# All of the first 21 slots' attention weights transposed by TensorE, and the loads on the GpSimd queue issued earlier

## The chip, the cores and the metric

The kernel runs on one core of a Trainium2 chip. The metric is the device time of one execution in microseconds; the kernel before took 562.66 us in the median of five runs (561.29 to 563.73). The engines are named as in the profile: PE (TensorE matmul), PEld (its weight loads), DVE (VectorE), ACT (ScalarE), POOL (GpSimd) and SP (SyncE, here only a queue that issues DMAs).

## The reference, cut to what matters

```python
def _attn_ref(q, k, v, tau):                      # (8, 8, 576, 64)
    scale = 1.0 / np.sqrt(q.shape[-1])
    scores = scale * np.matmul(q, k.transpose(0, 1, 3, 2))
    thresh = np.max(scores, axis=-1, keepdims=True) - tau
    scores = np.where(scores >= thresh, scores, -1000000000.0)
    scores = scores - np.max(scores, axis=-1, keepdims=True)
    attn = np.exp(scores)
    attn = attn / (np.sum(attn, axis=-1, keepdims=True) + 1e-09)
    return np.matmul(attn, v)

def _moe_ref(x, w_in, w_out):                     # (4608, 512), (512, 2048), (2048, 512)
    h = x @ w_in
    relu6 = np.clip(h + 3.0, 0.0, 6.0)
    g = h * relu6 / 6.0
    return g @ w_out
```

The output of the attention, with its heads side by side, is the input x of the second part. "Attention weights" below are the normalized `attn`; "projection weights" are w_in and w_out.

## The kernel before, in words

**Tiling.** The 64 heads are taken in 32 pairs; two pairs are a quad, two quads a batch. A quad has nine slots: slots 0 to 3 are the four blocks of 128 queries of its first pair, 4 to 7 those of its second, and slot 8 holds the remaining 64 queries of both. In a slot both heads of a pair are worked on, so every tile has two halves of 128 x 576. All 16 quads make a queue of 144 slots, numbered n = 0 to 143 here; n = 9 x quad + slot.

**One slot.** The loop at line 434 issues, in this order: the exponentials of the slot before (line 290, ACT); the row maxima of this slot (line 277, DVE, which also copies the scores out of PSUM) and the biases made of them (line 280, POOL, two tiny instructions); from n = 22 on a piece of the second part's first product (line 353 PE, 362 ACT or 364 DVE, 370 DVE); the transposes by TensorE of the slot two before, where it is marked `on_chip` (line 314, nine matmuls into the PSUM tile `pt`, one buffer of the pool `ps_h`, and line 315, their eviction on DVE); the reciprocal of the slot before (line 293, DVE); a piece of the second product (line 382); the masks of this slot (line 285, ACT); a transpose of q or k for the next pair or quad (line 213, 231) or a product with the values (`av`, lines 323 and 326); the scores of the next slot (lines 256 and 262, PE, into `ps_s`, two buffers); the warm-up (line 164, six PE transposes of an identity whose result nobody reads, n < 8); the normalization of the slot before (line 298, POOL, two instructions of 128 x 576); and at its end the transfers.

**Order.** The order is written out by hand. Every engine takes its instructions in the order of issue, so an instruction that waits holds all behind it on its engine. Where the eviction stands in the order of DVE is set by line 462: behind the reciprocal, ahead of the evictions of q and k.

**The two ways of a transpose.** The attention weights `pn` must be transposed before the product with v. A slot marked `on_chip` has it done by TensorE and DVE as told; any other slot gives one DMA transpose to SP's queue (line 306). In the kernel before the odd slots of the first 21 are marked: n = 1, 3, ... 19, ten slots.

**The queues.** SP's queue carries the loads of q and k (lists `loads`, one job a slot, each of several DMAs, lines 88, 92 and 107), the DMA transposes and the stores (line 403). POOL's queue carries what has to be cast to bf16 on the way: the values, four pieces a batch (list `vcasts`: two `vm` pieces of line 121 and two `vr` pieces of line 125), and the projection weights, 32 pieces (list `casts`: 16 of w_in, line 142, then 16 of w_out, line 146). POOL issues these in order with its biases and normalizations. The first batch's value pieces are in the list from the start; those of batch b + 1 are put there in slot 0 of the second quad of batch b, which is n = 9 for the second batch.

**When they are issued, before.** A value piece is started in a slot when n < 4 or n > 12, so the second batch's four go in slots 13 to 16. A weight piece is started in each slot from 4 to 23, and two in each slot from 24 to 29.

Of the kernel before, what the change touches and what calls it, by code (L numbers as in the profile page):

```python
# [21 lines left out]
def kernel(  # L22
# [20 lines left out]
    N1 = 22  # L43
# [31 lines left out]
    casts = []  # L75
    vcasts = []
# [3 lines left out]
    def load_quad(quad):  # L80
        b, g = divmod(quad, 2)
        nat[quad] = (nat_pool.tile([P, 1152], F32, tag="nq", name="nq"),
                     nat_pool.tile([P, 4, 4, D], F32, tag="km", name="km"),
                     nat_pool.tile([P, 2 * D], F32, tag="kr", name="kr"))
        nq, km, kr = nat[quad]

        def main(dst, src, h, order):
            nc.sync.dma_start(out=dst[:, :, h, :], in_=src[b, 4 * g + h, 0:512, :].rearrange(order, t=4))

        def blocks_q(n, a, j):  # L90
            c = 32 * (2 * a + j)
            nc.sync.dma_start(out=nq[c:c + 32, n * S:(n + 1) * S].rearrange("p (k d) -> p k d", d=32),
                              in_=q[b, 4 * g + 2 * n + a, :, 32 * j:32 * j + 32].rearrange("(k r) d -> r k d", r=32))

        def load_q(n):
            if b < NB:
                for a in range(2):
                    main(nq[:, 0:1024].rearrange("p (t h d) -> p t h d", h=4, t=4), q, 2 * n + a, "(t p) d -> p t d")
            else:
                for a in range(2):  # L100
                    for j in range(2):
                        blocks_q(n, a, j)

        def rest():
            for dst, src in ((kr[:], k), (nq[:, 1024:1152], q))[0:2 if b < NB else 1]:
                for n in range(2):
                    nc.sync.dma_start(out=dst[64 * n:64 * n + 64, :].rearrange("p (h d) -> p h d", h=2),
                                      in_=src[b, 4 * g + 2 * n:4 * g + 2 * n + 2, 512:S, :].rearrange("h p d -> p h d"))

        for n in range(2):  # L110
            loads.append(lambda n=n: [main(km, k, 2 * n + a, "(p t) d -> p t d") for a in range(2)])
            loads.append(lambda n=n: load_q(n))
            if n == 0:
                loads.append(rest)

    def load_v(b):
        vm = v_pool.tile([P, H, 4 * D], BF16, tag="vm", name="vm")
        vr = vrs[b % 2]
        vsb[b] = (vm, vr)
        for g in range(2):  # L120
            vcasts.append(lambda g=g: nc.gpsimd.dma_start(
                out=vm[:, g * 4:g * 4 + 4, :],
                in_=v[b, g * 4:g * 4 + 4, 0:512, :].rearrange("h (p t) d -> p h (t d)", t=4)))
        for a in range(2):
            vcasts.append(lambda a=a: nc.gpsimd.dma_start(
                out=vr[a * 64:(a + 1) * 64, a, :, :],
                in_=v[b, :, 512:S, :].rearrange("(hp a) p d -> a p hp d", a=2)[a]))
# [21 lines left out]
    def start(jobs, n):  # L149
        for _ in range(min(n, len(jobs))):  # L150
            jobs.pop(0)()
# [9 lines left out]
    def warm_up(count):  # L161
        warm = ps_h.tile([P, 2, 512], F32, tag="h", name="warm")
        for _ in range(count):
            nc.tensor.transpose(warm[:, 0, 0:P], identf[:], identf[:])
# [105 lines left out]
    def sm_max(sl):  # L270
        sl.s = s_pool.tile([P, 2, S], F32, tag="s", name="s")
        sl.m = stat_pool.tile([P, 2], F32, tag="m", name="m")
        sl.bias = stat_pool.tile([P, 2], F32, tag="bias", name="bias")
        sl.rsum = stat_pool.tile([P, 2], F32, tag="rsum", name="rsum")
        sl.rinv = stat_pool.tile([P, 2], F32, tag="rinv", name="rinv")
        for i, ps in enumerate(sl.tiles):
            nc.vector.tensor_scalar(out=sl.s[:, i, :].rearrange("p (a b) -> p a b", a=2), in0=ps[:, :, 0:HALF],  # L277
                                    scalar1=1.0, scalar2=None, op0=Alu.mult, op1=Alu.max,
                                    accum_out=sl.m[:, i:i + 1])
            nc.gpsimd.tensor_scalar(out=sl.bias[:, i:i + 1], in0=sl.m[:, i:i + 1], scalar1=-scale, scalar2=tau,  # L280
                                    op0=Alu.mult, op1=Alu.add)
# [6 lines left out]
    def sm_exp(sl, i):  # L288
        s = sl.s[:, i, :]
        nc.scalar.activation(out=s, in_=s, func=Act.Exp, accum_out=sl.rsum[:, i:i + 1])  # L290
# [67 lines left out]
    def mm1_relu(hps, on_act):  # L358
        w = hps.shape[2]
        r = r_pool.tile([P, 2, 320], F32, tag="r", name="r")[:, :, 0:w]  # L360
        if on_act:
            nc.scalar.activation(out=r, in_=hps, func=Act.Relu, bias=three[:])  # L362
        else:
            nc.vector.tensor_scalar(out=r, in0=hps, scalar1=3.0, scalar2=0.0, op0=Alu.add, op1=Alu.max)  # L364
        return r
# [58 lines left out]
    queue = []  # L424
    for quad in range(NQUAD):
        for slot in range(NSLOT):
            sl = Slot()
            sl.quad, sl.slot = quad, slot
            sl.on_chip = len(queue) < N1 - 1 and len(queue) % 2 == 1
            queue.append(sl)  # L430
    queue[0].tiles = scores(0, 0)

# [1 line left out]
    for n, sl in enumerate(queue):  # L434
        quad, slot = sl.quad, sl.slot
        b, g = divmod(quad, 2)
        now = n
        if slot in (0, 4):
            pts[2 * quad + slot // 4] = pt_pool.tile([P, 9, 512], BF16, tag="pT", name="pT")
        if slot == 8:  # L440
            ptr[quad] = ptr_pool.tile([P, 9, P], BF16, tag="pR", name="pR")
        if quad == 0 and slot == 0:
            load_quad(1)
        if slot == (4 if quad else 8) and quad + 2 < NQUAD:
            load_quad(quad + 2)
        if slot == 0 and g == 1 and b + 1 < B:
            load_v(b + 1)
        if prev is not None:
            for i in range(2):
                sm_exp(prev, i)  # L450
        sm_max(sl)

        if slot != 8 and todo1:
            item, then = todo1.pop(0)
            h = mm1(item)
            r = mm1_relu(h, on_act=(slot in (0, 1, 3, 5)))
            mm1_gate(item, h, r)
            todo2.extend(then)
        copies = pe_transpose(queue[n - 2]) if n > 1 and queue[n - 2].on_chip else None
        if prev is not None:  # L460
            sm_recip(prev)
        if copies:
            copies()
        outs = []


        pieces = 0 if slot == 3 else 1
        if slot == 0:
            second = True
        if second and slot < 2 and len(todo2) > 1 and todo2[0][1] == todo2[1][1]:  # L470
            pieces, second = 2, False
        for _ in range(pieces):
            if todo2:
                bb, mt, part = todo2.pop(0)
                mm2_part(bb, mt, part)
                if part == 3:
                    outs += mm2_out(bb, mt, on_act=False)
        for i in range(2):
            sm_mask(sl, i)
        evict = None  # L480
        nxt = 2 * quad + 2
        if slot == (1 if quad else 2):
            evict = transpose_q(2 * quad + 1)
        elif slot == (2 if quad else 3):
            evict = transpose_k(2 * quad + 1)
        elif slot == 3 and quad > 0:
            av_main(2 * quad - 1)
        elif slot == 4 and quad > 0:
            av_rest(quad - 1)
            if quad % 2 == 0:  # L490
                todo1.extend(moe_of(quad // 2 - 1))
        elif slot in (5, 6, 7) and quad + 1 < NQUAD:
            if slot == 5:
                alloc_qk(quad + 1)
                evict = transpose_q(nxt)
            elif slot == 6:
                evict = transpose_k(nxt)
            else:
                evict = transpose_rest(quad + 1)
        elif slot == 8:  # L500
            av_main(2 * quad)
        if evict:
            evict()
        if n + 1 < len(queue):
            queue[n + 1].tiles = scores(queue[n + 1].quad, queue[n + 1].slot)
        if n < 8:
            warm_up(6)
        if prev is not None:
            sm_norm(prev)
        flush()  # L510
        late.extend(outs)
        start(loads, 1)
        if n < 4 or n > 12:
            start(vcasts, 1)
        if n > 3:
            start(casts, 1 if n < 24 else 2)
        prev = sl

    for i in range(2):
# [66 lines left out]
```

## Time and profile before

| | us |
|---|---|
| median of five runs | 562.66 |
| lowest, highest | 561.29, 563.73 |
| profiled execution | 561.29 |
| its span, first to last instruction | 559.5 |
| span from slot 0's first maximum to slot 4's | 9.67 to 21.99 |
| slot 4's to slot 20's | 21.99 to 69.60 |
| slot 20's to slot 30's | 69.60 to 101.90 |
| last maximum of the queue's last slot | about 500 |

The span is the time from the first to the last instruction; 1.8 us lie around it. An engine's busy time says how long it worked, not what it waited for. In the groups of the profile a line gives source line, engine, operation, tiles, count, busy time and the mean of one in ns, and after the second bar the idle time of the engine ahead of them and what ended it. Some groups of the whole span on which the change bears:

```profile
L298 POOL TENSOR_SCALAR pn<-s,rinv 128x576 bf16<-128x576 f32 x288 | 212.4, 748 | 132.8 <-DVE rinv L293 59.5
L285 ACT ACTIVATE s<-s,bias 128x576 f32<-128x576 f32 x288 | 207.3, 768 | 34.6 <-POOL bias L280 33.6
...
L280 POOL TENSOR_SCALAR bias<-m 128x1 f32<-128x1 f32 x288 | 54.9, 191 | 65.6 <-DVE s L277 45.3
```

The timeline prints one line for each run of like instructions: start, length, engine, line, operation, tiles, count, and in brackets the idle time of the engine ahead of it with what ended it. A line without brackets followed its predecessor with next to no gap.

### The profile page before, as it was taken

What the parts mean: (1) busy time and instruction counts of PE and PEld (TensorE: products, weight loads), DVE (VectorE), ACT (ScalarE), POOL (GpSimd) and SP (SyncE); (2) the same over time, 40 slices, a digit from 0 to 9 for tenths busy, and PEclk for the clock granted to TensorE, in tenths of its full rate; (3) what the DMA queues carried; (4) which work ended last, traced back from release to release, by engine and by line L of the source; (5) the groups of instructions that cost most, each with busy time, mean ns of one, the idle gap of its engine ahead of it and who ended that gap; (6) DMA issues with size and microseconds to landing.
All of it is one profiled execution on the core that took longest, in us unless ns stands there. A gap on an engine that the chain in (4) does not pass through costs nothing.

```text
span 559.5 us, 11634 instructions
## 1 busy us (share of the span) xinstructions
PE 531.3 (95%) x3856; PEld 307.7 (55%) x3856; DVE 424.4 (76%) x1040; ACT 470.6 (84%) x999; POOL 306.7 (55%) x646
## 2 busy tenths in 40 slices
PE   7898798799999999999999999999999999999997
PEld 5565455555545565555555565655555555654663
DVE  3687786787878788887978798887978788883540
ACT  4899999798889999899889999899889999983540
POOL 1878878854566555754566555754566555561000
PEclk9999999999999999999999999999999999999999
DMA  5889999986789868988699867977699856453102
GB/s 111 136 121 173 170 166 189 194 150 126 137 165 143 160 126 162 175 147 147 131 153 164 162 121 159 179 147 148 131 145 166 167 119 124 100 109 83 38 20 76
DMA packets 286204, 77.52 MB, mean 139 GB/s; under 512 B 269248, under 2 KB 281536, under 8 KB 286144
## 3 DMA queue, kind: packets, MB, share of 16 engines
q1 hardware_dynamic: 268736, 67.86, 65.3%
q0 software_dynamic: 17408, 8.92, 14.0%
q8 instruction: 30, 0.49, 0.4%
q14 instruction: 30, 0.25, 0.2%
HBM read 36.70 MB, written 9.44 MB: 82 GB/s over the span
## 4 chain that ended last, share of the span: by engine, by line
PE 54%; DVE 11%; ACT 10%; issue 4%; SPq 2%; POOL 2%; DMA 2%; DVEq 0%; POOLq 0%
PE h L353 17%; PE o L382 16%; PE s L256 14%; DVE s L277 5%; ACT s L285 4%; ACT s L290 4%; PE av L323 3%; DVE g L370 2%; DVE r L364 2%; ACT r L362 2%; DMA nq<-in_q_dram 2%; POOL pn L298 1%; PE tp L213 1%; PE s L262 1%; PE ar L323 1%
## 5 line engine op out<-in xcount | busy, mean ns | idle before, releaser
L298 POOL TENSOR_SCALAR pn<-s,rinv 128x576 bf16<-128x576 f32 x288 | 212.4, 748 | 132.8 <-DVE rinv L293 59.5
L285 ACT ACTIVATE s<-s,bias 128x576 f32<-128x576 f32 x288 | 207.3, 768 | 34.6 <-POOL bias L280 33.6
L277 DVE TENSOR_SCALAR_CACHE_REDUCE s<-s 128x576 f32<-128x576 f32 x288 | 205.9, 752 | 40.2 <-PE s L256 29.9
L290 ACT ACTIVATE s<-s 128x576 f32<-128x576 f32 x288 | 193.1, 673 | 0.3
L256 PE MATMUL s<-kT,qT 64*128 64x288 f32 x1024 | 170.6, 430 | 5.9 <-DVE s L277 3.2
L353 PE MATMUL h<-xT,w_in_sb 128*128 128x320 bf16 (+1 forms) x1024 | 144.9, 287 | 6.1 <-DVE g L370 5.1
L382 PE MATMUL o<-w_out_sb,g 128*128 128x512 bf16 x576 | 140.9, 379 | 3.6 <-DVE osb L390 3.0
L353 PEld LDWEIGHTS <-w_in_sb 128*128 128x128 bf16 x1024 | 92.2, 97 | 69.0 <-issue 31.6
L370 DVE SCALAR_TENSOR_TENSOR g<-r,h 128x512 bf16<-128x512 f32 (+1 forms) x128 | 96.5, 755 | 42.1 <-ACT r L362 40.2
L256 PEld LDWEIGHTS s<-kT,qT 64*128 64x128 f32 x1024 | 93.9, 186 | 62.2 <-DVE s L277 24.9
L280 POOL TENSOR_SCALAR bias<-m 128x1 f32<-128x1 f32 x288 | 54.9, 191 | 65.6 <-DVE s L277 45.3
L382 PEld LDWEIGHTS <-g 128*128 128x128 bf16 x576 | 55.6, 98 | 58.2 <-issue 9.8
L362 ACT ACTIVATE r<-h,three 128x640 f32<-128x640 f32 (+1 forms) x74 | 54.5, 738 | 20.3 <-PE h L353 19.6
L290 ACT ACTIVATION_READ_ACCUMULATOR s<-s 128x1 f32 x288 | 54.7, 190 | 0.0
L364 DVE TENSOR_SCALAR r<-h 128x512 f32<-128x512 f32 (+1 forms) x54 | 40.6, 751 | 0.0
L390 DVE TENSOR_SCALAR osb<-o 128x512 f32<-128x512 f32 x31 | 21.0, 677 | 22.2 <-PE o L382 22.2
L323 PE MATMUL av<-pT,vm 128*64 128x512 bf16 x256 | 33.7, 385 | 2.1 <-ACT kT L203 2.0
L293 DVE RECIPROCAL rinv<-rsum 128x2 f32<-128x2 f32 x144 | 23.0, 160 | 11.7 <-ACT s L290 11.3
L323 PEld LDWEIGHTS <-vm 128*64 128x64 bf16 x512 | 17.8, 110 | 24.9 <-issue 17.7
L335 DVE CAST xT<-av 128x512 bf16<-128x512 f32 x32 | 21.8, 681 | 5.2 <-PE av L326 5.0
L277 DVE DVE_READ_ACCUMULATOR s<-s 128x1 f32 x288 | 24.0, 83 | 0.0
L388 ACT ACTIVATE osb<-o 128x512 f32<-128x512 f32 x5 | 3.0, 597 | 23.9 <-PE o L382 23.9
(42 smaller groups left out, 254.6 us busy)
## 6 DMA issues: line engine op xcount, KB each, us to landing
km<-in_k_dram SPq DMA_DIRECT2D x64, 128.0 KB, 3.0
out_dram<-osb SPq DMA_DIRECT2D x32, 256.0 KB, 2.4
nq<-in_q_dram SPq DMA_DIRECT2D x96, 72.0 KB, 2.7
vm<-in_v_dram POOLq DMA_DIRECT2D x16, 256.0 KB, 5.2
nq<-in_q_dram SPq DMA_DIRECT2D x16, 128.0 KB, 4.1
w_in_sb<-in_moe_w_in_dram POOLq DMA_DIRECT2D x16, 128.0 KB, 4.2
w_out_sb<-in_moe_w_out_dram POOLq DMA_DIRECT2D x16, 128.0 KB, 4.6
pT<-pn SPq DMA_TRANSPOSE x119, 3.4
```

The source lines that it names most:

```text
L256: nc.tensor.matmul(tiles[a][:, hf, 0:HALF], qT_of(pair)[a * 64:(a + 1) * 64, t * P:(t + 1) * P], keys(pair, a, hf), start=True, stop=True)
L277: nc.vector.tensor_scalar(out=sl.s[:, i, :].rearrange("p (a b) -> p a b", a=2), in0=ps[:, :, 0:HALF], scalar1=1.0, scalar2=None, op0=Alu.m ...
L280: nc.gpsimd.tensor_scalar(out=sl.bias[:, i:i + 1], in0=sl.m[:, i:i + 1], scalar1=-scale, scalar2=tau, op0=Alu.mult, op1=Alu.add)
L285: nc.scalar.activation(out=s, in_=s, func=Act.Prelu, bias=sl.bias[:, i:i + 1], scale=scale, alpha=REJECT)
L290: nc.scalar.activation(out=s, in_=s, func=Act.Exp, accum_out=sl.rsum[:, i:i + 1])
L298: nc.gpsimd.tensor_scalar(out=pn[:, i, :], in0=sl.s[:, i, :], scalar1=sl.rinv[:, i:i + 1], scalar2=1.0, op0=Alu.mult, op1=Alu.mult)
L323: nc.tensor.matmul(ps[a * 64:(a + 1) * 64, :], vm[:, 2 * hp + a, c * D:(c + 1) * D], pT[:, 5 * a + c, cols], start=(c == 0), stop=False)
L353: nc.tensor.matmul(hps[:, n, 0:w], w_in_sb[:, ki, (ni + n) * P:(ni + n + 1) * P], xT[b][:, ki, c0:c0 + w], start=(ki == 0), stop=(ki == KI ...
L362: nc.scalar.activation(out=r, in_=hps, func=Act.Relu, bias=three[:])
L364: nc.vector.tensor_scalar(out=r, in0=hps, scalar1=3.0, scalar2=0.0, op0=Alu.add, op1=Alu.max)
L370: nc.vector.scalar_tensor_tensor(out=gbuf[:, ni:ni + 2, c0:c0 + w], in0=r, scalar=6.0, in1=hps, op0=Alu.min, op1=Alu.mult)
L382: nc.tensor.matmul(o_ps[0], gbuf[:, ni, mt * P:(mt + 1) * P], w_out_sb[:, ni, :], start=(ni == 0), stop=(ni == NI - 1))
```

## The change

Three edits. All slots n = 0 to 20 are marked `on_chip`, not the odd ones alone: 21 slots are transposed by TensorE in place of ten, and eleven DMA transposes less are given to SP's queue. The warm-up groups of slots 0 to 7 are left out (those ahead of the loop stay). The two conditions on the transfers of POOL's queue are loosened: a value piece is started in any slot in which one is in the list, so the second batch's go in slots 9 to 12, and two weight pieces are started in every slot from 4 on, so that all 32 are issued in slots 4 to 19.

```diff
-            sl.on_chip = len(queue) < N1 - 1 and len(queue) % 2 == 1
+            sl.on_chip = len(queue) < N1 - 1
...
-        if n < 8:
-            warm_up(6)
         if prev is not None:
             sm_norm(prev)
         flush()
         late.extend(outs)
         start(loads, 1)
-        if n < 4 or n > 12:
-            start(vcasts, 1)
+        start(vcasts, 1)
         if n > 3:
-            start(casts, 1 if n < 24 else 2)
+            start(casts, 2)
```

`N1` is 22.

## The prediction

> **What bounds the kernel now.** I read the engine totals first. They point at TensorE, but the change only touches the first 30 of the 144 slots, so I then cut the span by slots, found by counting pairs of the row maxima of line 277 (slot 0 starts at 9.67 us, slot 4 at 21.99, slot 20 at 69.60, slot 30 at 101.90). The stretches run from the first bias of slot 4 to that of slot 20, and from there to that of slot 30.
>
> ```profile
> PE 531.3 (95%) x3856; PEld 307.7 (55%) x3856; DVE 424.4 (76%) x1040; ACT 470.6 (84%) x999; POOL 306.7 (55%) x646
> ...
> 22.85:70.61 47.76, 42.17 (x327) 25.12 (x328) 38.26 (x106) 43.83 (x95) 40.77 (x84) 1.00 1.12 155
> 70.61:106.50 35.89, 30.14 (x225) 18.70 (x226) 25.36 (x69) 31.45 (x70) 29.10 (x59) 1.00 1.17 180
> ```
>
> Columns of the last two: stretch, length, busy time of PE, PEld, DVE, ACT, POOL, granted clock, DMA share, GB/s. In the first stretch a slot takes 47.76 / 16 = 2.98 us. ACT is busy 43.83 us; its own work for a slot (two masks 1.44, two exponentials 1.33) is 2.77. POOL is close behind with 40.77, and it is the engine to which the change gives work here: every weight or value piece is issued on POOL, in order with the bias and the normalization. The POOL timeline shows what a slot with two pieces costs:
>
> ```profile
> 49.02 0.46 POOL L280 TENSOR_SCALAR bias<-m 128x1 f32<-128x1 f32 x2
> 49.57 1.48 POOL L298 TENSOR_SCALAR pn<-s,rinv 128x576 bf16<-128x576 f32 x2
> 50.99 0.80 POOL L121 DMA_DIRECT2D vm<-in_v_dram  x1
> 51.79 0.54 POOL L142 DMA_DIRECT2D w_in_sb<-in_moe_w_in_dram  x1
> 52.41 0.46 POOL L280 TENSOR_SCALAR bias<-m 128x1 f32<-128x1 f32 x2
> ...
> 87.42 0.46 POOL L280 TENSOR_SCALAR bias<-m 128x1 f32<-128x1 f32 x2
> 87.98 1.48 POOL L298 TENSOR_SCALAR pn<-s,rinv 128x576 bf16<-128x576 f32 x2
> 89.39 1.12 POOL L146 DMA_DIRECT2D w_out_sb<-in_moe_w_out_dram  x2
> 90.59 0.46 POOL L280 TENSOR_SCALAR bias<-m 128x1 f32<-128x1 f32 x2
> ```
>
> There is no idle time marked on any of these lines: POOL goes round back to back. From bias to bias it is 52.41 - 49.02 = 3.39 us with a value and a weight piece, and 90.59 - 87.42 = 3.17 us with two weight pieces. Both are longer than ACT's 2.77, and ACT shows who is late, here in slots 14, 15 and 24, 25, 28, 29:
>
> ```profile
> 52.62 1.44 ACT L285 ACTIVATE s<-s,bias 128x576 f32<-128x576 f32 x2 [0.61 <-POOL bias L280]
> 56.01 1.44 ACT L285 ACTIVATE s<-s,bias 128x576 f32<-128x576 f32 x2 [0.61 <-POOL bias L280]
> ...
> 83.82 1.44 ACT L285 ACTIVATE s<-s,bias 128x576 f32<-128x576 f32 x2 [0.69 <-POOL bias L280]
> 87.64 1.44 ACT L285 ACTIVATE s<-s,bias 128x576 f32<-128x576 f32 x2 [0.56 <-POOL bias L280]
> 98.99 1.44 ACT L285 ACTIVATE s<-s,bias 128x576 f32<-128x576 f32 x2 [1.40 <-POOL bias L280]
> 102.91 1.44 ACT L285 ACTIVATE s<-s,bias 128x576 f32<-128x576 f32 x2 [1.15 <-POOL bias L280]
> ```
>
> The piece issues stand directly ahead of the late bias. From 130 to 205 us TensorE is busy 72.98 of 75 us, and so on to the end; the instructions there are the same before and after, so whatever the first 30 slots lose or gain moves the end by as much.
>
> **The change, slots 0 to 3.** The warm-up groups (0.87 us each in the timeline) go; the transposes of slots 0 and 1 now sit in slots 2 and 3 instead of one in slot 3 alone. Slot 2 gets nine transposes (0.66 us in PE) and one eviction (0.74 us, line 315) between the reciprocal at 16.23 and the q eviction, so the maximum of slot 3 moves from 17.15 to about 17.8. ACT is still busy with slot 2's exponentials until 19.06, which hides it. Value +0.2 us; ends -0.9 (a warm-up group was on the path) and +1.5 (two evictions uncovered).
>
> **Slots 4 to 19: two pieces in every slot.** The 32 weight pieces, now one a slot from 4 to 23 and two a slot to 29, are all issued by slot 19; the second batch's four value pieces move from slots 13-16 to 9-12 and come as a third piece. POOL's round is 3.17 us in 12 slots, 3.17 + 0.80 in two (vm) and 3.17 + 0.66 in two (vr, 0.66 us in the timeline): 38.04 + 7.94 + 7.66 = 53.64 us for what takes 47.76. That is +5.9 us, because the late bias holds the mask on ACT, behind it the exponentials, behind these the reciprocal on VectorE, and that is what the next normalization on POOL waits for.
>
> **The transposes in these slots.** Eight more slots of the stretch get nine transposes and a 0.74 us eviction. On PE they stand ahead of the q and k transposes and the next scores; they wait for the normalization two slots back and for the one bank `pt`, freed by the eviction a slot earlier. VectorE per slot becomes about 1.44 (two maxima) + 0.17 + 0.74 + 0.67 (a q or k eviction) = 3.0 us: under POOL's 3.17, by little. The nearest rows are slots 15 and 17, which have both two pieces and a transpose now: around them POOL keeps its cadence (biases at 55.80, 59.06, 62.32: 3.26 each). So mostly hidden. In the three slots that also hold `av` (1.2 us of PE) the scores come some 0.3 us late by the same counting: I take +0.8. Ends: 0, and +8.7 (slots with a transpose now last 3.60 on average, those without 2.51; if each of eight paid the whole difference of 1.09). The eleven DMA transposes that go leave SP's queue: the k and q loads behind them are issued earlier, but TensorE waits for a load only 0.9 us in all, so 0 here.
>
> **Slots 20 to 30: pieces gone.** Of ACT's waits above, the removed issues account for 0.58 (at 83.82), 0.56, 1.07 (two w_out pieces at 97.62) and 1.07 (at 101.55): 3.3 us. ACT's busy share is highest here, so most of it comes through; VectorE's chain takes some back. Value -2.7; ends -3.3 and 0. Cover for landing early: w_in is first read at 78.55, w_out at 108.38, both later than the last piece in either kernel. Two new transposes (in slots 20, 22) cost VectorE 0.74 each, beside ACT: +0.4, ends 0 and +1.5.
>
> **Slots 30 to 38: lighter DMA.** The chain of waits (start, length, what) has a q load on it:
>
> ```profile
> 128.53 0.56 SPq L92
> ...
> 129.68 2.70 DMA nq<-in_q_dram
> ```
>
> With the w_out casts out of 84 to 106 us, where the DMA share is over 1, SP's backlog of transposes may be shorter here. Value -0.5 (most of a late load's 2.7 us is its own time); ends -2.7 and 0.
>
> **Sum.** 0.2 + 5.9 + 0.8 - 2.7 + 0.4 - 0.5 = +4.1 us. The profiled execution took 561.29 us (span 559.5 and 1.8 around it); the changed one would take 565.4 (span 563.6). That execution is the fastest of five, 1.37 under their median of 562.66; on the median the forecast is 566.8.
>
> **A rule against the change.** The granted clock is 1.00 in every stretch I asked for, from the first microsecond on, with transposes as the only PE work until 7.8 us. The Trainium skill, "TensorE: Matmul & The Clock Gate", Part 4, says that PE transposes do not count as busy for the clock gate and that an idle window brings half clock. By it the early slots, now fuller of transposes, could run slow; but the warm-ups that go are transposes too, and the row shows no slow clock even where they were alone. By the row the term is 0; by the rule it would be the third rival's.
>
> **Rivals.** *Not slower, by the later stage:* what speeds up is worth more than I take. The pieces that leave slots 20 to 29 are 4 x 0.58 + 6 x 1.1 = 8.9 us of POOL; were POOL the pace there, the balance would be 0.2 + 5.9 - 8.9 = -2.8, 559.9 us. Against it: ACT is busy 31.45 of 35.89 us there, so at most 4.4 can come back. With that and the whole 2.7 of the q load: 0.2 + 5.9 - 4.4 - 2.7 = -1.0, 561.7. Faster: 0.15; the band of no change round 562.66: 0.09. *VectorE and TensorE pace the slots instead of POOL:* every slot of 4 to 19 costs the 3.60 of today's transpose slots, 57.6 instead of 47.76, +9.8; with the other terms +7.2, 569.9. For it: VectorE's 3.0 per slot lies just under the pace. Against: those 3.60 already hold waits for ACT. 0.18. *The chip's clock gates TensorE* once the warm-ups are gone: eight slots with 1.24 us of scores doubled, +9.9 on top, 576.7. Only the missing idle stretches speak against it. 0.04. My forecast (+1.2 to +6): 0.54.
>
> **Range.** The likeliest case reaches from 563.9 to 569. The forecast range takes in the second rival and the edge of the first: 561.2 to 573. A measurement of this kernel can tell about 0.2% (1.1 us) from no change. Faster 0.15, within 0.09, slower 0.76.
>
> **What would show it.** POOL lines without idle time from 23 to 76 us and a bias-to-bias time of 3.17 (3.8 to 4.0 in slots 9 to 12); the stretch from slot 4's to slot 20's first bias 53 to 56 us; no ACT wait for the bias behind a w_out piece after that; slots 20 to 29 some 2 to 3 us shorter; 3907 matmuls, 1051 VectorE instructions, 123 DMA transposes; clock 1.00. If the stretch is under 50 us, POOL's round was mispriced; if slots 4 to 19 are longer than 56 with idle POOL, the second rival is right; if all of this holds and the end still doesn't move, the PE-bound stage is where it went.

## The result, and the profile after

The changed kernel takes 564.76 us in the median (23 executions, 564.0 to 566.88), the kernel before 562.61 (44). The ratio is 1.0039, interval 1.0031 to 1.0048: slower by 2.2 us (1.7 to 2.7). The profiled executions are 564.03 against 561.29, +2.7. The forecast was +4.1.

The engine totals of the kernel after, and two stretches of its span (from slot 4's first bias to slot 20's, from there to slot 30's; columns as before):

```profile
PE 529.9 (94%) x3907; PEld 306.0 (54%) x3907; DVE 431.2 (77%) x1051; ACT 470.5 (84%) x999; POOL 306.9 (55%) x646
...
22.82:76.95 54.13, 42.39 (x376) 25.05 (x378) 43.84 (x117) 44.42 (x96) 49.40 (x100) 1.00 0.79 123
76.95:109.05 32.10, 29.17 (x230) 18.51 (x228) 25.81 (x69) 30.36 (x66) 20.64 (x43) 1.00 0.70 115
```

The totals hardly move. The stretches do: the first is 6.4 us longer (47.76 before), the second 3.8 shorter (35.89). POOL's busy time went from 40.77 to 49.40 in the first and from 29.10 to 20.64 in the second: about 8.5 us of issues were moved. They paced the first stretch nearly throughout, and the second only in some of its slots. POOL's timeline in slot 4, and in slots with two and with three issues:

```profile
22.82 0.19 POOL L280 TENSOR_SCALAR bias<-m 128x1 f32<-128x1 f32 x1 [1.36 <-DVE s L277]
23.49 0.19 POOL L280 TENSOR_SCALAR bias<-m 128x1 f32<-128x1 f32 x1 [0.48 <-DVE rinv L293]
...
26.43 0.46 POOL L280 TENSOR_SCALAR bias<-m 128x1 f32<-128x1 f32 x2
...
29.60 0.46 POOL L280 TENSOR_SCALAR bias<-m 128x1 f32<-128x1 f32 x2
30.15 1.48 POOL L298 TENSOR_SCALAR pn<-s,rinv 128x576 bf16<-128x576 f32 x2
31.57 1.12 POOL L142 DMA_DIRECT2D w_in_sb<-in_moe_w_in_dram  x2
32.77 0.46 POOL L280 TENSOR_SCALAR bias<-m 128x1 f32<-128x1 f32 x2
...
43.23 0.46 POOL L280 TENSOR_SCALAR bias<-m 128x1 f32<-128x1 f32 x2
43.78 1.48 POOL L298 TENSOR_SCALAR pn<-s,rinv 128x576 bf16<-128x576 f32 x2
45.20 0.80 POOL L121 DMA_DIRECT2D vm<-in_v_dram  x1
46.00 1.07 POOL L142 DMA_DIRECT2D w_in_sb<-in_moe_w_in_dram  x2
47.15 0.46 POOL L280 TENSOR_SCALAR bias<-m 128x1 f32<-128x1 f32 x2
```

From bias to bias it is 3.17 us with two issues and 3.92 with three, with no idle time marked; in slot 4, where POOL comes out of an idle time, it is 3.61. The chain of waits, followed back from the last instruction, runs mostly through POOL in this stretch; a part of it (start, length, what):

```profile
26.98 1.47 POOL pn L298 x2
28.46 0.52 POOL w_in_sb L142
28.98 0.54 POOL w_in_sb L142
29.60 0.10 POOL bias L280
29.70 0.17 issue
29.86 0.20 POOL bias L280
30.15 1.48 POOL pn L298 x2
```

And ACT's masks, the bias of which comes late, in slots 6, 7, 10 and 13, and then in 28 and 29:

```profile
29.81 1.44 ACT L285 ACTIVATE s<-s,bias 128x576 f32<-128x576 f32 x2 [0.39 <-POOL bias L280]
32.98 1.45 ACT L285 ACTIVATE s<-s,bias 128x576 f32<-128x576 f32 x2 [0.39 <-POOL bias L280]
...
43.45 1.44 ACT L285 ACTIVATE s<-s,bias 128x576 f32<-128x576 f32 x2 [1.35 <-POOL bias L280]
...
54.98 1.44 ACT L285 ACTIVATE s<-s,bias 128x576 f32<-128x576 f32 x2 [1.03 <-POOL bias L280]
...
102.95 1.44 ACT L285 ACTIVATE s<-s,bias 128x576 f32<-128x576 f32 x2 [0.33 <-POOL bias L280]
106.19 1.44 ACT L285 ACTIVATE s<-s,bias 128x576 f32<-128x576 f32 x2 [0.46 <-POOL bias L280]
```

The mask of each slot from 5 to 20 waits: 0.39 us behind two pieces (0.82 behind the first two), 1.03 to 1.35 behind three. In all, ACT's masks wait 10.6 us for their bias in the first stretch, against 4.9 before (in both, 1.24 of it is slot 4's own wait, behind no weight piece); in the second it is 1.6 against 4.3.

How far each slot's first maximum (line 277, VectorE) and first mask (line 285, ACT) start behind those of the kernel before, worked out from both timelines:

| slot | 4 | 8 | 12 | 16 | 20 | 22 | 28 | 30 | 31 | 47 | 90 | 143 |
|---|---|---|---|---|---|---|---|---|---|---|---|---|
| maximum, us | -0.03 | +0.42 | +2.46 | +5.48 | +5.37 | +6.08 | +5.03 | +4.77 | +3.27 | +3.26 | +3.26 | +2.91 |
| mask, us | -0.03 | +1.31 | +4.76 | +5.22 | +6.30 | +6.08 | +3.96 | +3.19 | +3.26 | +3.26 | +3.26 | +2.90 |

The loss is made by slot 20, most of it in slots 8 to 16, with the value pieces of slots 9 to 12 as its steepest part. Nearly half comes back: ACT's masks are 6.08 us behind in slots 22 and 23 and 3.28 in slot 29, and the maxima follow by slot 31. From there the distance stands at 3.26 but for slots 96 to 100. At slot 124 another 0.35 us comes back for good; the chain of the kernel before has 0.42 us "issue" ahead of that maximum, the changed one 0.07, and the profiles show no cause.

### The profile page after: what moved, and what is told of

The parts are those of the page before. It is cut to its first block, busy times and chain, and to the rows that moved or that the text cites. A ratio compares the mean times of both kernels' runs of the same rounds, so it can differ in the third digit from the quotient of the medians.

```text
span 562.3 us, 11722 instructions
## 1 busy us (share of the span) xinstructions
PE 529.9 (94%) x3907; PEld 306.0 (54%) x3907; DVE 431.2 (77%) x1051; ACT 470.5 (84%) x999; POOL 306.9 (55%) x646
## 4 chain that ended last, share of the span: by engine, by line
PE 60%; DVE 12%; ACT 8%; POOL 7%; issue 3%; DMA 3%; SPq 2%; DVEq 0%; POOLq 0%
PE o L382 17%; PE h L353 17%; PE s L256 17%; DVE s L277 5%; POOL pn L298 4%; PE av L323 4%; ACT s L285 3%; ACT s L290 3%; DMA nq<-in_q_dram 3%; DVE g L370 2%; DVE r L364 2%; ACT r L362 2%; PE s L262 1%; PE tp L213 1%; POOL bias L280 1%
## 5 line engine op out<-in xcount | busy, mean ns | idle before, releaser
L256 PE MATMUL s<-kT,qT 64*128 64x288 f32 x1024 | 167.8, 430 | 3.5 <-DVE kT L201 1.5
L256 PEld LDWEIGHTS s<-kT,qT 64*128 64x128 f32 x1024 | 92.3, 186 | 58.3 <-DVE s L277 20.8
L314 PE MATMUL pt<-identb,pn 128*128 128x128 bf16 x189 | 17.5, 221 | 12.9 <-POOL pn L298 12.7
L314 PEld LDWEIGHTS <-pn 128*128 128x128 bf16 x189 | 10.7, 98 | 25.3 <-POOL pn L298 24.5
```

The costliest lines, as they stand in the source:

```text
L256: nc.tensor.matmul(tiles[a][:, hf, 0:HALF], qT_of(pair)[a * 64:(a + 1) * 64, t * P:(t + 1) * P], keys(pair, a, hf), start=True, stop=True)
```

## The experiments

**One part at a time.** Four kernels, each with one part of the change or without one: the pieces alone, the transposes alone, the warm-ups alone, and the change with the old times of the pieces.

```diff
# e1_pieces, to the kernel before
-        if n < 4 or n > 12:
-            start(vcasts, 1)
+        start(vcasts, 1)
...
-            start(casts, 1 if n < 24 else 2)
+            start(casts, 2)
# e2_transposes, to the kernel before
-            sl.on_chip = len(queue) < N1 - 1 and len(queue) % 2 == 1
+            sl.on_chip = len(queue) < N1 - 1
# e3_nowarm, to the kernel before
-        if n < 8:
-            warm_up(6)
# e4_old_pieces, to the changed kernel: e1's lines undone
```

> Only the two conditions on POOL's transfers are changed; odd slots alone are transposed by TensorE and the warm-ups stay. POOL theory (the round of bias, normalization and two pieces paces slots 4 to 19): bias of slot 4 to bias of slot 20 takes 53 to 55 us (47.8 before, 54.1 with the whole change), slots 20 to 30 come back by about 3, and the whole time is 2 to 3 us over the kernel before (ratio 1.003 to 1.006), as with the whole change. Rival (VectorE and TensorE pace the slots once every slot has transposes): the stretch stays under 51 us, and with the later slots relieved the time is that of before or less (ratio 0.996 to 1.001).

> Only the marking of slots is changed: all of the first 21 are transposed by TensorE; warm-ups and the old times of the pieces stay. POOL theory: POOL's round with one piece is 2.60 us, so the slots are held by ACT (2.77) and VectorE (about 3.0); bias of slot 4 to bias of slot 20 takes 47.5 to 50 us (47.8 before), ratio 1.000 to 1.003. Rival (the transposes pace): 52 us or more, ratio 1.004 to 1.010.

> Only the warm-up groups of slots 0 to 7 are left out. POOL theory: no more than 0.3 us either way up to slot 20, granted clock 1.00, ratio 0.999 to 1.001. Rival (the clock gate): a granted clock under 1 in the first 30 us and several us more up to slot 8, ratio 1.005 or more.

> The changed kernel with the old times of the pieces put back (every slot of the first 21 transposed by TensorE, no warm-ups in the loop). POOL theory: the slowdown is gone but for what the transposes cost, bias of slot 4 to bias of slot 20 takes 47.5 to 50 us (54.1 with the whole change), ratio to the kernel before 0.999 to 1.003. Rival (the transposes pace): the stretch stays at 52 us or more and, with the later slots again burdened by pieces, the time is over that of the changed kernel (ratio 1.006 to 1.012).

| | median us | ratio to before, interval | slot 4 to 20 | slot 20 to 30 |
|---|---|---|---|---|
| before | 562.70 | | 47.76 | 35.89 |
| e1, pieces alone | 566.41 | 1.0060 (1.0034 to 1.0086) | 54.72 | 32.10 |
| e2, transposes alone | 563.77 | 1.0011 (0.9997 to 1.0025) | 49.69 | 35.87 |
| e3, no warm-ups | 562.29 | 0.9992 (0.9976 to 1.0009) | 49.12 | 35.87 |
| e4, change with old pieces | 564.15 | 1.0014 (0.9995 to 1.0033) | 48.34 | 35.88 |

The stretches are from the profile of one execution each. Those of e1, and the first of e4:

```profile
25.07:79.79 54.72, 45.47 (x332) 26.81 (x333) 38.80 (x109) 44.39 (x96) 49.38 (x100) 0.94 1.16 179
79.79:111.89 32.10, 28.44 (x219) 17.81 (x215) 24.50 (x67) 30.35 (x66) 20.64 (x43) 1.00 0.86 138
...
25.00:73.34 48.34, 42.19 (x373) 25.65 (x374) 43.09 (x114) 43.65 (x95) 40.72 (x84) 1.00 0.59 94
```

The pieces alone carry both the loss and what comes back: POOL's busy time is 49.38 as with the whole change, while VectorE's is the 38 of the kernel before. Without them (e4) neither is there. That the DMA engines were the cause is unlikely: their share in the first stretch is 1.16 in e1 and 0.79 with the whole change, and the stretch is as long in both. e1's whole time is more than its two stretches explain (+7.0 and -3.8): its slot 4 already starts 2.2 us late at half clock, and all its eight executions have a mean granted clock of 0.990 or less. The transposes cost up to 1.9 us in the stretch; on the whole time the median does not tell that from none, but e2's three executions at a clock of 0.999 took 562.7 us and the three of the kernel before at 0.999 or more 561.1 to 561.7, so some 1.3 us may be real where POOL is not the pace. Leaving out the warm-ups makes no measurable difference. That a granted clock of 0.94 stands in e1's first stretch, and half speed in e3's early slots, belongs to single executions; it is taken up at the end.

**The price by itself: the same bytes in fewer issues.** In the changed kernel, the two weight pieces of a slot become one DMA.

```diff
# e5_merged, to the changed kernel (w_out likewise)
+            for ki in range(0, KI, 2):
+                casts.append(lambda n4=n4, ki=ki: nc.gpsimd.dma_start(
+                    out=w_in_sb[:, ki:ki + 2, n4 * 512:(n4 + 1) * 512],
+                    in_=moe_w_in[ki * P:(ki + 2) * P, n4 * 512:(n4 + 1) * 512].rearrange("(a p) f -> p a f", p=P)))
...
-            start(casts, 2)
+            start(casts, 1)
```

> The changed kernel with the same bytes in the same slots, but the two weight pieces of a slot as one DMA of twice the size. If POOL's issue is paid per instruction (a vm piece of twice a weight piece's bytes took 0.80 us against 0.57), POOL's round falls from 3.17 to 2.7 to 2.9 us, and by the POOL theory bias of slot 4 to bias of slot 20 falls from 54.1 to 48 to 51 us, with slots 20 to 30 as fast as with the change: ratio to the kernel before 0.995 to 1.000. Rival one (issue is paid by size): round and time as with the change, ratio 1.003 to 1.006. Rival two (bytes or landings on the DMA engines, not POOL's issue, hold the slots): the round of POOL shows idle time, the stretch stays at 53 us or more.

558.75 us, ratio 0.9942 (0.9919 to 0.9966). POOL's timeline in this kernel:

```profile
26.11 0.45 POOL L281 TENSOR_SCALAR bias<-m 128x1 f32<-128x1 f32 x2
26.66 1.47 POOL L299 TENSOR_SCALAR pn<-s,rinv 128x576 bf16<-128x576 f32 x2
28.07 0.76 POOL L142 DMA_DIRECT2D w_in_sb<-in_moe_w_in_dram  x1
28.91 0.45 POOL L281 TENSOR_SCALAR bias<-m 128x1 f32<-128x1 f32 x2
```

The bytes of both pieces are issued in 0.76 us (0.73 in the mean of the 16), in place of 1.12 for two pieces, and the round falls from 3.17 to 2.80, ACT's pace. The two stretches:

```profile
22.90:72.23 49.33, 42.38 (x374) 25.89 (x374) 43.38 (x114) 44.19 (x95) 43.29 (x84) 1.00 0.85 136
72.23:104.35 32.12, 29.62 (x232) 18.94 (x230) 26.14 (x71) 30.57 (x68) 20.54 (x44) 1.00 0.69 114
```

The same transposes in the same slots, the same bytes at the same places, no warm-ups as in the change, and a DMA share of 0.85 against 0.79: of POOL's work 6.1 us of issues went, and 4.8 us of the first stretch with them; the ratio is a little under the lower end expected. This is the run that shows POOL's issue time to be the price of the change.

**The kernel before, with its pieces placed better.** e6 keeps the 32 single pieces and spreads them; e7 takes the merged ones, with no slot from 4 to 26 that has two issues.

```diff
# e6_spread, to the kernel before
+    gate = singles.tile([P, 1], F32)
+    nc.gpsimd.tensor_scalar(out=gate[:], in0=nat[0][0][:, 1151:1152], scalar1=1.0, scalar2=0.0,
+                            op0=Alu.mult, op1=Alu.add)
+    start(vcasts, 4)
...
-        if n < 4 or n > 12:
+        if n > 12:
             start(vcasts, 1)
-        if n > 3:
-            start(casts, 1 if n < 24 else 2)
+        if not (13 <= n <= 16 or 27 <= n <= 30):
+            start(casts, 2 if n in (2, 3, 21, 22, 23, 31, 32) else 1)
# e7_best, to the kernel before, with e5's merged pieces
-        if n < 4 or n > 12:
+        if n < 4 or n > 19:
             start(vcasts, 1)
...
-            start(casts, 1 if n < 24 else 2)
+            start(casts, 1)
```

> The kernel before with its pieces spread so that fewer slots hold two: the first batch's values issued once the first q load has landed, ahead of slot 0; weight pieces from slot 0 on, none in slots 13 to 16 and 27 to 30 where a value piece is issued, two in slots 2, 3, 21, 22, 23, 31 and 32. POOL theory: the waits of ACT behind a second piece (2.2 us in slots 14 to 17, 3.3 us in 24 to 29) go, and 2 to 5 us of the whole time with them: ratio 0.991 to 0.997. Rival (other engines take up the slack at once): within 0.2% of before.

> The kernel before with weight pieces merged in twos (16 DMAs), one in each of slots 4 to 19, and the second batch's values in slots 20 to 23, so that no slot up to 26 holds two issues; odd slots transposed by TensorE and warm-ups as before. POOL theory: round 2.7 to 2.9 in slots 4 to 19, near ACT's 2.77, so bias of slot 4 to bias of slot 20 takes 46 to 49 us (47.8 before) and slots 20 to 30 come back by about 3 (32.1 against 35.9): ratio 0.990 to 0.996. Rival (issue is paid by size): the stretch takes 52 us or more, ratio 1.002 to 1.006.

e6: 559.38 us, ratio 0.996 (0.9935 to 0.9984); first stretch 46.24, second 33.23. e7: 560.22 us, 0.9962 (0.9941 to 0.9984); 47.08 and 33.20. Both as the POOL theory has it: the same engines, the same work, and 0.7 to 2.7 us out of each stretch by where POOL's issues stand and, in e7, by how few they are. e7 lies just over the upper edge of what was expected.

**Fewer issues still, and where that ends.** Pieces merged in fours, in every second slot, odd slots transposed by TensorE.

```diff
# e8_fours, to e7_best (w_out likewise)
+            casts.append(lambda n4=n4: nc.gpsimd.dma_start(
+                out=w_in_sb[:, :, n4 * 512:(n4 + 1) * 512],
+                in_=moe_w_in[:, n4 * 512:(n4 + 1) * 512].rearrange("(a p) f -> p a f", p=P)))
...
-        if n > 3:
+        if n > 3 and n % 2 == 0:
             start(casts, 1)
```

> As the run with pieces merged in twos and no slot with two issues (e7), but merged in fours: eight weight DMAs, in slots 4, 6, ... 18. From 0.57 us for one piece and 0.74 for two, a line gives 0.40 + 0.17 per piece, so about 1.08 us for four. POOL theory: POOL then needs 2 x 2.05 + 1.08 = 5.2 us for two slots, under ACT's 5.5, so nothing more is won than e7 has won: ratio 0.991 to 0.996, the maximum of slot 20 at most 1 us earlier than in e7 counted from slot 4. Rival (POOL's issue is still the pace in e7): another 1.5 us or more off that stretch.

563.07 us, ratio 1.0006 (0.999 to 1.0023): nothing is left of e7's gain, which neither theory had. Up to slot 20 it is as expected (46.70 us in the first stretch); four pieces are issued in 0.79 us, so an issue is nearly a price per instruction, not the line through 0.57 and 0.74 that I drew. Then slots 20 to 30 take 37.20. The timeline in slot 21:

```profile
75.12 1.92 PE L323 MATMUL av<-pT,vm 128*64 128x512 bf16 x8 [2.51 <-DMA pT<-pn]
...
77.50 0.69 DVE L335 CAST xT<-av 128x512 bf16<-128x512 f32 x1 [3.71 <-PE av L326]
...
80.30 1.45 ACT L285 ACTIVATE s<-s,bias 128x576 f32<-128x576 f32 x2 [4.40 <-POOL bias L280]
```

A DMA transpose is late for the product with the values, and everything behind it on TensorE waits. It is no accident of one execution: the least of e8's twelve times is 561.49, that of e7's is 557.8. So e8 was run again with the other half of the change, all first 21 slots transposed by TensorE, and with the value pieces in the slots that have no weights.

```diff
# e10_fours_pe, to e8_fours
-            sl.on_chip = len(queue) < N1 - 1 and len(queue) % 2 == 1
+            sl.on_chip = len(queue) < N1 - 1
...
-        if n < 4 or n > 19:
+        if n < 4 or n % 2 or n > 19:
             start(vcasts, 1)
```

> Weight pieces merged in fours as in the run before, in slots 4, 6, ... 18, the second batch's values in slots 9, 11, 13, 15, so that no slot up to 26 holds two issues; and, as in the change, all of the first 21 slots transposed by TensorE (warm-ups as before). In e8 a DMA transpose landed late in slot 21 (TensorE idle 2.5 us for it, ACT 4.4 us). Theory (POOL's issues were the price of the change, and the transposes by TensorE take the late landings out of this stage): bias of slot 4 to bias of slot 20 takes 47 to 50 us (54.1 with the change), no wait for a DMA transpose before slot 24, slots 20 to 30 about 32 us: ratio 0.990 to 0.996. Rival (the loss in slot 21 comes from the large pieces themselves or the q and k loads, not from the DMA transposes): a like loss of 3 us or more in slots 8 to 24, ratio 0.998 or more. Rival two (the transposes pace): the stretch over 52 us.

558.58 us, ratio 0.9934 (0.9908 to 0.9959): 48.06 us in the first stretch, 32.64 in the second, no wait for a DMA transpose up to slot 30. It and e5 have the lowest medians of this study, and beat both kernels. A part of their lead is the clock of their executions (0.999 and 0.997 in the mean, 0.994 to 0.995 for the kernel before on their chips): at 0.999 or more the kernel before took 560.9 to 561.4 us, the change 564.0 to 564.1, e5 558.6 to 558.8, e10 558.5 to 558.6, and e7's two fastest executions, at 0.999 and 0.998, took 557.8 and 557.9, though one at 1.000 took 559.6. The loss in slot 21 went with the DMA transposes; as the value pieces moved too, that it went by them alone is likely, not shown. That the big pieces delay a transpose, rather than the q load that SP issues next to it (two DMAs, 3.14 us at 68.13), is not separated either.

**The warm-ups as matmuls.** In the kernel before, all warm-ups made of twice as many bf16 matmuls with the identity.

```diff
# e9_warm_mm, to the kernel before (the identity's bf16 copy made ahead of it)
-        for _ in range(count):
-            nc.tensor.transpose(warm[:, 0, 0:P], identf[:], identf[:])
+        for _ in range(2 * count):
+            nc.tensor.matmul(warm[:, 0, 0:P], identb[:], identb[:], start=True, stop=True)
```

> The kernel before with its warm-ups (all of them) made of twice as many bf16 matmuls with the identity in place of fp32 transposes. In the runs so far the granted clock of one execution (0.98 to 1.00 in the mean, half speed for some us in the first slots) goes with its time, about 3.5 us for 0.01. If transposes do not count as work for the clock gate and matmuls do, most executions have a mean clock of 0.998 or more and the median falls by 1 to 1.5 us: ratio 0.997 to 0.999. Rival (the warm-ups make no difference to the clock, whatever they are): mean clock about 0.995 as before, ratio 0.999 to 1.001.

562.95 us, ratio 1.0011 (0.9993 to 1.0029), mean granted clock 0.993 over 12 executions against 0.995 over 22 of the kernel before on the same chip. The first theory falls.

## Why the prediction was right, and by how much it was off

**The bound.** That POOL, not the transposes, would pace slots 4 to 19: shown, by e1 (pieces alone make the loss), e4 (without them it is gone) and e5 (with half the weight issues, at the same bytes, three quarters of it are gone).

**Slots 0 to 3.** +0.2 forecast, -0.03 measured. The eviction added in slot 2 moved slot 3's maximum to 17.53 and was hidden behind ACT's exponentials, as the text said.

**Slots 4 to 19.** POOL's rounds were summed to 53.64 us, the stretch measured 54.13: +6.4 of the +6.7 forecast with the 0.8 for the transposes. The rounds of 3.17 repeat to the hundredth; those with three issues were 3.8 to 4.1. The odd half microsecond is slot 4's round, 3.61 in place of 3.17: its second bias comes 0.67 us behind the first, waiting for VectorE. In slot 9, where the chain runs through `av`, the round is 0.15 over its sum, and the three behind it are 0.1 under theirs. The transposes were hidden, as the rows of slots 15 and 17 had suggested; alone, with POOL out of the way, they cost 1.9 (e2) or 0.6 (e4 less the kernel before).

**Slots 20 to 30.** The text took -2.7 for the pieces and +0.4 for two more transposes. The three measures of the table and the profile differ here: the stretch is 3.8 us shorter by POOL's biases, 3.1 by ACT's masks, and slots 20 to 31 are 2.1 closer by VectorE's maxima. ACT is the engine that the removed issues held up, so its masks tell it best. In slots 22 and 23 they are 6.08 us behind; in slots 24, 25, 28 and 29 they regain 0.57, 0.48, 1.07 and 0.68 us, where the text had summed waits of 0.58, 0.56, 1.07 and 1.07. That is 2.8 us for the 2.7 forecast. The slot 30 that falls from 6.14 to 4.64 us is no further gain: there TensorE's `av` waits for ACT's key copy, 2.0 us before and 0.3 after, and that copy is 3.27 us behind, as the mask ahead of it is.

**The terms that were mis-sized.** They are the transposes. By slot 23, ahead of the first wait that was removed, the text had 0.2 + 5.9 + 0.8 + 0.4 = +7.3 us; measured are 6.08, POOL's 5.9 and next to nothing else. The +0.8 was added to a stretch that POOL paced and in which VectorE and TensorE had time to spare (busy 43.84 and 42.39 of 54.13 us); the +0.4 stood for slots 20 and 22, through which ACT's masks lose nothing (6.30, 6.13 and 6.08 behind in slots 20 to 22).

**Slots 30 to 38.** -0.5 forecast, nothing measured: the table stands still from slot 31 to slot 90. The q load is still on the chain (2.80 us at 132.87, where it was 2.70 at 129.68).

**The sum.** On the profiled executions +2.7 against +4.1: the forecast was 1.2 too high up to slot 23 and missed the 0.35 that came back at slot 124, but it took off 0.5 for a q load that gained nothing; the rest is 0.3. So the errors cancel in part, and that the sum lay no further off is to that extent luck. The medians differ by 2.2.

**The rivals.** VectorE and TensorE as the pace: fallen with e2. Its price was also read too high: the 3.60 and 2.51 are means over slots 3 to 21 and 4 to 22; over slots 4 to 19 alone it is 3.41 with a transpose and 2.54 without. The not-slower rival asked for 4.4 us from ACT and 2.7 from the q load; ACT gave 2.8 and the q load nothing. The clock: no loss of time from leaving out the warm-ups (e3), although its executions have a mean granted clock of 0.992 (12), the kernel before on that chip 0.995 (31).

## What to carry to other kernels

On POOL here, DMA issues stand in order with the engine's own work and take its time. Where a computing engine issues DMAs, write its round for a slot as busy times plus issues, and compare it with the slowest other engine before moving issues from one stage to another; the same 8.5 us cost 6.1 to 6.4 in the stage that they paced and gave back 2.8 to 3.8 in the one that they left, by the engine on which it is measured. Where that round is the pace, fewer and bigger DMAs come first (0.57 us for one piece, 0.73 for two in one, 0.79 for four), and spreading them second. And costs on engines that are not the pace of a stage are not added to it; forecast and measurement are compared on the engine that is.

## What the runs showed of the hardware that had not been expected

An issue on POOL costs far more by instruction than by bytes: 128 KB of destination in 0.57 us, 256 KB in 0.73, 512 KB in 0.79; the `vm` piece, of 256 KB too, 0.80, and the small `vr` piece (32 KB) 0.65.

The granted clock differs between executions of one kernel, and in the changed kernel it goes with the time: executions with a mean clock of 0.999 or more took 564.0 to 564.1 us, those of 0.991 to 0.993 566.2 to 566.9. It is no rule: of e9's executions four at 0.990 took 562.6, and one at 0.997 took 566.5. The windows (start and end, length, busy PE, PEld, DVE, ACT, POOL, granted clock, DMA share, GB/s) of e1, which has all its warm-ups:

```profile
8.00:12.00 4.00, 3.35 (x14) 1.80 (x15) 1.66 (x5) 1.80 (x4) 0.96 (x3) 0.87 0.76 173
12.00:16.00 4.00, 4.00 (x16) 2.49 (x16) 1.61 (x5) 3.74 (x10) 2.13 (x5) 0.50 0.51 66
16.00:20.00 4.00, 4.00 (x26) 2.60 (x23) 2.30 (x7) 2.41 (x5) 2.23 (x6) 0.77 0.63 74
20.00:24.00 4.00, 2.94 (x27) 2.07 (x26) 2.79 (x7) 3.68 (x10) 3.48 (x7) 1.00 1.08 175
```

Half the clock from about 11 to 18 us, and slot 4's first bias 2.2 us later than in the kernel before. The Trainium skill, "TensorE: Matmul & The Clock Gate", Part 4, has it that transposes do not count as activity for the gate; the run with matmuls in their place (e9) had no better clock, so the reason is open. Half speed was also seen in mid-kernel: in e9's profiled execution (the one of 566.5) TensorE waited 4.1 us for a DMA transpose in slot 31, and the granted clock was 0.59 from 114 to 118 us, right behind it; in e8 it was 0.70 from 76 to 80, behind the wait of slot 21.
